# A KV-cache decode kernel: the last kept unit of a row's first pass moves behind all units scored ahead, ten of twelve V's instead of twelve run ahead of the kept K's, fewer V's are loaded in halves, and there are five sets of p

## The chip, the cores and the metric

The kernel runs on one core of a Trainium2 chip. The metric is device microseconds of one execution. A core has TensorE (PE; its weight loads are shown as PEld), VectorE (DVE), ScalarE (ACT), GpSimd (POOL) and SyncE (SP), and 16 DMA engines that move data between HBM and the on-chip SBUF. In this kernel SP issues almost all loads; it waits in order, so a load whose target is not yet free holds back all loads behind it.

## The reference

There are 8 batch rows, each with one token of 448 values. Two layers run one after the other with the same weights and the same K and V caches: attention, MLP block, attention, MLP block. In short:

```
def A(x):                                   # attention over the cache
    q = (x @ wq).reshape(8, 1, 16, 256)
    scores = einsum("bhqd,bhkd->bhqk", q, repeat(k_cache, 2)) * 256 ** -0.5
    o = einsum("bhqk,bhkd->bhqd", softmax(scores), repeat(v_cache, 2))
    return o.reshape(8, 1, 4096) @ wo
def B(x):                                   # one token: the shifted mixer adds nothing
    x1 = x + hs                             # hs comes from rows of zeros
    return x1 + gelu(layernorm(x1) @ w3) @ w4
x = x + A(layernorm(x)); x = x + B(layernorm(x))
x = x + A(layernorm(x)); x = x + B(layernorm(x))
```

Each cache is (8 rows, 8 KV heads, 4096 positions, 256 values) in bf16, 134 MB. K and V of every row are needed twice, once in each pass, and a row's second pass needs its query, which depends on everything in its first pass. Rows don't depend on one another.

## The kernel before

**Units and items.** A unit (called a task in the code) is a pass (0 or 1), a row and a pair `gp` (0 to 3) of two KV heads. It has four K pieces and four V pieces of 1 MB each. The kernel writes out by hand one list, `items`, of 512 such pieces in the order in which they are used. A K item is transposed in 32x32 blocks on VectorE (`transpose_k`, L777) and multiplied with the query on TensorE (`scores`, L792; two K pieces that lie side by side are scored with one set of 32 matmuls instead of two); ScalarE then takes exponentials (L801). A V item is multiplied with the probabilities on TensorE (`pv`, L845, 16 matmuls). Before its first V, a unit's probabilities are transposed by four matmuls and a copy (`turn_p`, L828 and L835) into one of `NP` sets (`psv`, L114), and ScalarE copies the part for each V into `ptw` (L955).

**Places.** SBUF has 15 places of 1 MB. Pairs 2 and 3 are "kept": for the row in progress all eight K pieces and four V pieces of these two units stay in their places from the first pass to the second, and one V plus a quarter of another is set aside in PSUM (L812, L1086). At the moment when the first pass ends, 12 of 15 places are held and only three are left to stream through. `emit_loads` walks the load list in the order of `items` after each item and issues whatever has a place; `place_for` and `both_for` choose the place and hold two neighbours for the two halves of a K pair, in which case the second waits for its own place even if others are free. A V in the set `halved` is loaded as two DMAs of half a MB (L767), every other as one (L764); a pair of K's whose two places are both to be had goes as one DMA of 2 MB (L739).

**The chain of a row.** Between a row's first and second pass stand: denominators of the softmax, scaling of the output (L476), the product with wo (L365), a norm (L235, L254), the MLP (L383, L365), another norm, the product with wq (L316) and the spreading of the query (L335). It is a generator, advanced a step at a time by `step`. So that loads go on meanwhile, units of other rows, whose queries are there already, are scored ahead, and their V's are left over (`due`). The first `AFTER` = 12 of these go into `items` right behind the first pass; they are called `narrow`. While a narrow V is used, one step of the chain is taken in the middle of its 16 matmuls and one after them. A step that yields 2 makes the chain skip one turn, if the item is in `loose`. Here the three free places are a ring: a place is loaded, used and loaded again.

**The order.** `block(k, v)` puts the four K's of unit k and among them what is due. `first_kept` (L581 on) writes the first pass of a row's two kept units k2 and k3 together with the units scored ahead (four of them, so 16 V's, in rows 0 to 3; three, so 12 V's, in rows 4 to 7). In it, the last unit scored ahead comes after k3. The second pass then begins with the kept K's, which need no load; scoring two of them frees two places. V's that are due beyond the twelve stand among these.

Of the kernel before, what the change touches and what calls it, by code (L numbers as in the profile page):

```python
# [8 lines left out]
FP32 = mybir.dt.float32  # L9
BF16 = mybir.dt.bfloat16  # L10
U32 = mybir.dt.uint32
ACT = mybir.ActivationFunctionType
ALU = mybir.AluOpType
# [4 lines left out]
def kernel(  # L18
# [27 lines left out]
    nc = tc.nc  # L46
# [5 lines left out]
    Hq = HD // Dh  # L52
# [5 lines left out]
    HC = F // 128  # L58
    scale_exp = float(Dh) ** -0.5

    NC = 15
    NP = 4

    kept = [(gp, 0, n) for gp in (GP - 1, GP - 2) for n in range(4)]
    kept += [(GP - 1, 1, n) for n in range(1, 4)] + [(GP - 2, 1, 2)]
# [6 lines left out]
    chn = ctx.enter_context(tc.tile_pool(name="chn", bufs=1))  # L72
# [10 lines left out]
    MID = Bn // 2  # L83
# [126 lines left out]
    def norm(x, nb, twice):  # L210
# [19 lines left out]
        nc.vector.tensor_reduce(  # L230
            xs, xx.rearrange("p s f b -> p s b f"), mybir.AxisListType.X, ALU.add
        )
        yield 2
        st = room_ps("st", nb).rearrange("p (s b) -> p s b", b=nb)
        nc.tensor.matmul(st, ones, xs, start=True, stop=True)  # L235
        yield 0
# [71 lines left out]
    def project_q(b0, nb, qT):  # L308

        yield from norm(xT[:, :, b0 : b0 + nb], nb, False)  # L310
        q_ps = room_ps("q", nb).rearrange("p (c b) -> p c b", b=nb)
        for j in range(2):
            for h in range(Hq):
                for fc in range(4):
                    w, xi = wblk(wq_sb, HD, 2 * h + j, fc)
                    nc.tensor.matmul(  # L316
                        q_ps[:, j * Hq + h, :],
                        w,
                        xbs(nb)[:, xi, :],
                        start=(fc == 0),  # L320
                        stop=(fc == 3),
                    )
                if h % 8 == 7:
                    yield (2, 0)[j] if h == Hq - 1 else None
        nc.vector.tensor_copy(qT, q_ps)  # L325
        yield

# [48 lines left out]
    def mlp_hidden(b0, nb):  # L376

        yield from norm(xT[:, :, b0 : b0 + nb], nb, True)
        h_ps = room_ps("h", nb)
        for c in range(HC):  # L380
            for fc in range(4):
                w, xi = wblk(w3_sb, F, c, fc)
                nc.tensor.matmul(  # L383
                    h_ps[:, c * nb : c * nb + nb],
                    w,
                    xbs(nb)[:, xi, :],
                    start=(fc == 0),
                    stop=(fc == 3),
                )
            if c % 7 == 6:  # L390
                yield 0 if c == HC - 1 else None
        g_t = chn.tile([128, 2, HC * MID], FP32, tag="g")
        hh, g0 = g_t[:, 0, 0 : HC * nb], g_t[:, 1, 0 : HC * nb]
        if nb == 1:
            HT_t = chn.tile([128, HC, 1], BF16, tag="HT")
            HT = HT_t[:]
        else:
            HT = HTw[:, :, b0 : b0 + nb]

        nc.vector.tensor_scalar_mul(hh, h_ps, 0.5)  # L400
        nc.vector.scalar_tensor_tensor(g0, hh, 2 * 0.044715, h_ps, ALU.mult, ALU.mult)
        nc.vector.scalar_tensor_tensor(g0, g0, 1.0, h_ps, ALU.add, ALU.mult)
        nc.scalar.activation(g0, g0, ACT.Tanh, scale=0.7978845608028654)
        yield 0
        nc.vector.scalar_tensor_tensor(
            HT,
            g0.rearrange("p (c b) -> p c b", b=nb),
            1.0,
            hh.rearrange("p (c b) -> p c b", b=nb),
            ALU.add,  # L410
            ALU.mult,
        )
        yield 2
        return HT
# [150 lines left out]
    AFTER = 12  # L565
# [21 lines left out]
    def first_kept(b, units, before):  # L587

        k2, k3 = ((0, b, gp) for gp in keep)
        todo = list(units)  # L590
        block(todo.pop(0), before)
        if len(todo) > 2:
            block(todo.pop(0))
        block(k2)
        block(todo.pop(0), k2) if todo else block(None, k2)
        block(k3)
        block(todo.pop(0), k3) if todo else block(None, k3)
        assert not todo
        items.extend(due)
        due.clear()  # L600
        for u in units:
            due.extend((number[u], 1, c) for c in range(4))
        narrow.update(due)
        if len(due) >= AFTER:
            loose.update(due)
        halved.update(due[: AFTER + 2])
        items.extend(due[:AFTER])
        del due[:AFTER]

    block((0, 0, free[0]))  # L610
    block((0, 0, free[1]), (0, 0, free[0]))
# [284 lines left out]

    def add_gen(kind, g, at=0, until=0, total=0, main=False):
        gens.append(
            {"kind": kind, "g": g, "at": at, "until": until, "n": 0, "of": total, "skip": 0, "main": main}
        )  # L900

    alone = []
# [1 line left out]
    def step(idx, calm=False, kinds=("chain", "last", "rest")):  # L904

        for kind in kinds:
# [3 lines left out]
            if alone and idx < len(items) and kind != "rest" and not e.get("locks"):  # L910
                if kind == "last" or not any(m["main"] for m in gens):
                    continue
            if calm and e["skip"] and items[now[0]] in loose:
                e["skip"] -= 1
                continue
            if not e["of"] or e["n"] < e["of"] * (idx - e["at"] + 1) / max(e["until"] - e["at"], 1):
                e["n"] += 1
                had = len(locked)
                got = next(e["g"], gens)
                while calm and got == 0:  # L920
                    got = next(e["g"], gens)
                if len(locked) != had:
                    e["locks"] = len(locked) > had
                e["skip"] = 1 if got == 2 else 0
                if got is gens:
                    gens.remove(e)

# [242 lines left out]
```

## Time and profile before

| | |
|---|---|
| Time, median of 3 runs | 1092.21 us (1091.31 to 1095.92) |
| The profiled execution: its own time | 1093.14 us |
| The profiled execution: span | 1091.3 us |
| Mean granted TensorE clock | 0.586 |
| Moved by DMA | 438.29 MB, 402 GB/s on average |
| Busy: PE, PEld, DVE, ACT, POOL | 673.7, 421.5, 605.6, 160.5, 16.3 us |

No engine is busy for more than 62% of the span, while the load queue of SP is busy for 98.3% of it, as the mean of 16 DMA engines. The row of GB/s in 40 slices of the span is the one to read: it moves between 374 and 427 in the body of the kernel, and where it dips there are chains. A window of a few microseconds gives the same number for any stretch.

### The profile page before, as it was taken

Reading aid. Unit: us, or ns where it says so; the run is one execution under the profiler, and the core shown is the slowest. Engines: PE = TensorE matmul, PEld = TensorE weight load, DVE = VectorE, ACT = ScalarE, POOL = GpSimd, SP = SyncE. Lnnn points to the kernel's source line nnn. Section 1 sums busy time; section 2 is a strip of 40 time slices with the busy share of each in tenths; the row PEclk is TensorE's granted clock in tenths of the full one; section 3 lists DMA queues with packets and bytes.
Section 4 is the critical chain, followed back from the end, with each engine's and each line's share of the span. In section 5 each row is a group of like instructions: output and inputs, shape, how many; then the busy total and the mean of one; then the engine's idle time right before and its main releaser. Section 6 shows DMA issues by size and latency. Waiting matters only on the chain.

```text
span 1091.3 us, 30928 instructions
## 1 busy us (share of the span) xinstructions
PE 673.7 (62%) x13836; PEld 421.5 (39%) x13836; DVE 605.6 (55%) x1266; ACT 160.5 (15%) x612; POOL 16.3 (1%) x27
## 2 busy tenths in 40 slices
PE   3244457943777348764587537764776467756785
PEld 2122234522445124432254324542454244533555
DVE  4357841597318872288623873289327941795181
ACT  0011111211112111111101211111111111111120
POOL 0000000000000000000000000000000000000000
PEclk9995555565556555565555655556556555655565
DMA  9999999999999999999999999999999999999994
GB/s 357 394 427 426 420 393 398 419 425 426 374 411 424 425 408 393 402 425 420 398 393 420 421 423 385 395 418 426 392 382 422 423 380 377 426 416 394 400 420 186
DMA packets 71509, 438.29 MB, mean 402 GB/s; under 512 B 7624, under 2 KB 11600, under 8 KB 40016
## 3 DMA queue, kind: packets, MB, share of 16 engines
q1 hardware_dynamic: 71184, 435.94, 98.3%
q8 instruction: 108, 1.77, 0.6%
q10 hardware_dynamic: 192, 0.38, 0.1%
q14 instruction: 25, 0.20, 0.0%
HBM read 436.28 MB, written 0.01 MB: 400 GB/s over the span
## 4 chain that ended last, share of the span: by engine, by line
DMA 61%; PE 19%; DVE 13%; SPq 3%; issue 2%; ACT 2%; POOL 0%; DVEq 0%; ACTq 0%
DMA places<-in_A_v_cache_dram 40%; DMA places<-in_A_k_cache_dram 19%; DVE places L777 10%; PE sc L792 8%; PE o L845 6%; SPq L174 2%; PE misc L365 2%; DVE store L812 1%; PE misc L476 1%; SPq L764 1%; ACT p_n L801 1%; DVE places L819 1%; DMA wq_sb<-in_A_wq_dram 1%; PE misc L383 1%; PE misc L316 1%
## 5 line engine op out<-in xcount | busy, mean ns | idle before, releaser
L777 DVE STREAM_TRANSPOSE places<-places 128x512 uint32<-128x512 uint32 (+1 forms) x576 | 456.5, 854 | 87.2 <-DMA places<-in_A_k_cache_dram 79.0
L792 PE MATMUL sc<-places,qbd 128*8 128x128 bf16 (+1 forms) x5440 | 257.8, 342 | 228.4 <-DVE places L777 215.9
L845 PE MATMUL o<-places,ptw 128*8 128x256 bf16 x3968 | 253.7, 385 | 145.6 <-DMA places<-in_A_v_cache_dram 113.7
L792 PEld LDWEIGHTS <-qbd 128*8 128x8 bf16 x5440 | 139.7, 106 | 304.6 <-DVE places L777 137.8
L845 PEld LDWEIGHTS <-ptw 128*8 128x8 bf16 x3968 | 99.7, 99 | 226.4 <-issue 135.3
L801 ACT ACTIVATE p_n<-sc 128x256 bf16<-128x256 f32 x128 | 95.1, 743 | 390.6 <-PE sc L792 390.6
L955 ACT COPY ptw<-psv 128x32 bf16<-128x32 bf16 x248 | 50.1, 225 | 187.9 <-PE o L845 163.3
L440 DVE RECIPROCAL rz<-misc 128x8 f32<-128x8 f32 (+1 forms) x35 | 6.4, 184 | 101.7 <-PE misc L437 44.3
L835 ACT CAST psv<-misc 128x128 bf16<-128x128 f32 x64 | 17.0, 265 | 267.9 <-PE misc L828 267.9
L365 PEld LDWEIGHTS <-wo_sb 128*128 128x128 bf16 x1280 | 38.8, 105 | 17.7 <-issue 17.5
L316 PEld LDWEIGHTS <-wq_sb 128*128 128x128 bf16 x1152 | 33.6, 104 | 24.0 <-issue 13.9
L476 PE MATMUL misc<-R_t,o_sb 128*128 128x8 f32 (+1 forms) x132 | 30.7, 342 | 11.4 <-ACT o_sb L470 5.9
L472 DVE MEMSET o<- 128x256 f32 x33 | 9.0, 272 | 49.8 <-PE o L845 39.2
L476 PEld LDWEIGHTS misc<-R_t,o_sb 128*128 128x128 f32 x132 | 27.9, 293 | 21.5 <-ACT o_sb L470 12.3
L339 DVE CAST qbd<-misc 32x64 bf16<-32x64 f32 x104 | 22.4, 215 | 22.0 <-PE misc L335 20.9
L801 ACT ACTIVATION_READ_ACCUMULATOR p_n<-sc 128x1 f32 x128 | 33.7, 264 | 0.0
L365 PE MATMUL misc<-OT,wo_sb 128*128 128x1 bf16 x1024 | 31.9, 166 | 2.5 <-DVE zs_t L426 2.5
L316 PE MATMUL misc<-xb,wq_sb 128*128 128x1 bf16 x1024 | 32.6, 166 | 0.3 <-issue 0.3
L325 DVE CAST qT<-misc 128x32 bf16<-128x32 f32 x8 | 1.5, 192 | 55.0 <-PE misc L316 55.0
L254 POOL TENSOR_TENSOR t<-t,nhalf 128x2 f32<-128x2 f32 (+2 forms) x20 | 14.0, 703 | 1062.4 <-DVE t L275 1062.4
L437 PEld LDWEIGHTS misc<-zm,one 128*128 128x128 f32 x70 | 16.0, 285 | 12.1 <-issue 7.5
L383 PEld LDWEIGHTS <-w_sb 128*128 128x128 bf16 x560 | 16.8, 105 | 10.0 <-issue 9.5
(104 smaller groups left out, 313.5 us busy)
## 6 DMA issues: line engine op xcount, KB each, us to landing
places<-in_A_k_cache_dram SPq DMA_DIRECT2D x53, 2048.0 KB, 21.1
places<-in_A_v_cache_dram SPq DMA_DIRECT2D x210, 512.0 KB, 7.4
places<-in_A_v_cache_dram SPq DMA_DIRECT2D x103, 1024.0 KB, 17.2
places<-in_A_k_cache_dram SPq DMA_DIRECT2D x86, 1024.0 KB, 13.9
places<-in_A_v_cache_dram SPq DMA_DIRECT2D x8, 768.0 KB, 7.5
wo_sb<-in_A_wo_dram SPq DMA_DIRECT2D x1, 3584.0 KB, 27.0
wq_sb<-in_A_wq_dram SPq DMA_DIRECT2D x3, 1024.0 KB, 9.6
w_sb<-in_B_w_dram SPq DMA_DIRECT2D x1, 1568.0 KB
```

What stands on the lines that cost most here:

```text
L174: nc.sync.dma_start(t[:, fc * cols : (fc + 1) * cols], src[fc * 128 : fc * 128 + 128, :])
L316: nc.tensor.matmul(q_ps[:, j * Hq + h, :], w, xbs(nb)[:, xi, :], start=(fc == 0), stop=(fc == 3),)
L339: nc.vector.tensor_copy(qbd[32 * a : 32 * a + 32, :, :, a, :], qs.rearrange("p e (f g u h) -> p (e f) u g h", f=2, u=2, h=2)[:, :, u],)
L365: nc.tensor.matmul(y_ps[:, fc, :], w[:, i, at : at + 128], rhs(i), start=start, stop=stop, skip_group_check=open is not None,)
L383: nc.tensor.matmul(h_ps[:, c * nb : c * nb + nb], w, xbs(nb)[:, xi, :], start=(fc == 0), stop=(fc == 3),)
L476: nc.tensor.matmul(ot_ps[:, j], o_sb[:].rearrange("p (i j) -> p j i", j=2)[:, j], R, start=True, stop=True)
L777: nc.vector.transpose(w, w)
L792: nc.tensor.matmul(sc[32 * k : 32 * k + 8, 128 * x : 128 * (x + nx)], qbd[:, ep, gp].rearrange("p a h -> p (a h)"), v, start=(n == 0), sto ...
L801: nc.scalar.activation(p_sb[:, :, :, 2 * u : 2 * u + 2].rearrange("p t i x -> p x t i"), sc[:, 256 * u : 256 * u + 256].rearrange("p (x t ...
L835: nc.scalar.copy(p_to, pt_ps.rearrange("p t k (a h) -> p a (t k) h", a=4))
L845: nc.tensor.matmul(o_ps[32 * q : 32 * q + 8, :], ptz[:, at : at + 8], v[:, y * Dh : (y + 1) * Dh], start=False, stop=(y >= 12), skip_group ...
L955: nc.scalar.copy(ptw[:, ring_of[it], :, 6:8], psv[slot_of[it[0]]][:, it[2]])
```

## The change

The order in `first_kept` changes: all units scored ahead now stand before k3, the last kept unit, whose four K's and four V's are the last loads before the ring. The number n of V's put right behind the first pass is the smaller of 12 and two less than are due: 12 of 16 in rows 0 to 3 as before, and 10 of 12 in rows 4 to 7, where the other two now stand behind the first two kept K's of the second pass. Only the first n - 2 of the V's ahead are loaded in halves: 10 instead of 14 in a row of 16, 8 instead of 12 in a row of 12. More units hold probabilities at once, so there are five sets of p; the room comes from the MLP's scratch tile `g`, whose second part moves, for four rows at once, into PSUM. The MLP's two products now read the halved value from SBUF twice instead of the original from PSUM, with the constants changed accordingly. Skipped turns are renumbered: a step that yields 2 always skips the next, one that yields 3 only in `loose`, which now holds only where n is 12. The steps that yield 3 are the norm before its matmul and the second of four parts of the product with wq.

```
-    NP = 4
+    NP = 5
...
         block(k2)
-        block(todo.pop(0), k2) if todo else block(None, k2)
+        block(todo.pop(0), k2)
+        if todo:
+            block(todo.pop(0))
+        assert not todo
         block(k3)
-        block(todo.pop(0), k3) if todo else block(None, k3)
-        assert not todo
-        items.extend(due)
-        due.clear()
+        block(None, k3)
         for u in units:
             due.extend((number[u], 1, c) for c in range(4))
+        n = min(AFTER, len(due) - 2)
         narrow.update(due)
-        if len(due) >= AFTER:
+        if n == AFTER:
             loose.update(due)
-        halved.update(due[: AFTER + 2])
-        items.extend(due[:AFTER])
-        del due[:AFTER]
+        halved.update(due[: n - 2])
+        items.extend(due[:n])
+        del due[:n]
...
-        yield 2
+        yield 3
...
-                    yield (2, 0)[j] if h == Hq - 1 else None
+                    yield (3, 0)[j] if h == Hq - 1 else None
...
-            if calm and e["skip"] and items[now[0]] in loose:
-                e["skip"] -= 1
+            if calm and e["skip"]:
+                e["skip"] = False
                 continue
...
-                e["skip"] = 1 if got == 2 else 0
+                e["skip"] = got == 2 or (got == 3 and items[now[0]] in loose)
...
-        g_t = chn.tile([128, 2, HC * MID], FP32, tag="g")
-        hh, g0 = g_t[:, 0, 0 : HC * nb], g_t[:, 1, 0 : HC * nb]
+        g_t = chn.tile([128, HC * MID], FP32, tag="g")
+        hh = g_t[:, 0 : HC * nb]
+        g0 = g_t[:, HC : 2 * HC] if nb == 1 else misc[:, 448 : 448 + HC * nb]
...
-        nc.vector.scalar_tensor_tensor(g0, hh, 2 * 0.044715, h_ps, ALU.mult, ALU.mult)
-        nc.vector.scalar_tensor_tensor(g0, g0, 1.0, h_ps, ALU.add, ALU.mult)
-        nc.scalar.activation(g0, g0, ACT.Tanh, scale=0.7978845608028654)
+        nc.vector.scalar_tensor_tensor(g0, hh, 4 * 0.044715, hh, ALU.mult, ALU.mult)
+        nc.vector.scalar_tensor_tensor(g0, g0, 1.0, hh, ALU.add, ALU.mult)
+        nc.scalar.activation(g0, g0, ACT.Tanh, scale=2 * 0.7978845608028654)
```

More of the change, by code (lines that the diff above doesn't have):

```diff
@@ L898, in add_gen @@
         gens.append(
-            {"kind": kind, "g": g, "at": at, "until": until, "n": 0, "of": total, "skip": 0, "main": main}
+            {"kind": kind, "g": g, "at": at, "until": until, "n": 0, "of": total, "skip": False, "main": main}
         )
```

## The prediction

> **What bounds the kernel now.** First the page: queue, chain and issues.
>
> ```profile
> DMA  9999999999999999999999999999999999999994
> GB/s 357 394 427 426 420 393 398 419 425 426 374 411 424 425 408 393 402 425 420 398 393 420 421 423 385 395 418 426 392 382 422 423 380 377 426 416 394 400 420 186
> q1 hardware_dynamic: 71184, 435.94, 98.3%
> ...
> DMA 61%; PE 19%; DVE 13%; SPq 3%; issue 2%; ACT 2%; POOL 0%; DVEq 0%; ACTq 0%
> ...
> places<-in_A_v_cache_dram SPq DMA_DIRECT2D x210, 512.0 KB, 7.4
> places<-in_A_v_cache_dram SPq DMA_DIRECT2D x103, 1024.0 KB, 17.2
> ```
>
> The queue is full throughout, yet its rate dips to 374 to 400 at regular distances. The question is what one MB costs in the dips. So next the table of stretches, around the chains of row 1 (first three), row 4 (next four) and row 6 (columns: stretch, length, busy time of PE, PEld, DVE, ACT, POOL, granted clock, DMA share, GB/s):
>
> ```profile
> 195.00:265.00 70.00, 43.29 (x864) 26.15 (x864) 56.79 (x93) 11.90 (x43) 0.00 (x0) 0.57 1.01 424
> 265.00:295.00 30.00, 16.02 (x296) 9.42 (x296) 12.98 (x30) 4.05 (x17) 0.70 (x1) 0.56 0.97 381
> 295.00:320.00 25.00, 19.58 (x413) 11.56 (x407) 3.75 (x21) 2.76 (x13) 0.55 (x1) 0.50 1.03 412
> 580.00:650.00 70.00, 40.49 (x841) 25.45 (x830) 49.13 (x84) 11.77 (x44) 0.00 (x0) 0.60 1.01 422
> 650.00:670.00 20.00, 12.50 (x234) 7.41 (x235) 10.04 (x20) 3.18 (x15) 0.00 (x0) 0.59 0.96 377
> 670.00:690.00 20.00, 15.66 (x340) 9.63 (x335) 4.04 (x24) 2.02 (x10) 1.25 (x2) 0.50 1.03 409
> 690.00:725.00 35.00, 26.23 (x594) 19.34 (x586) 16.90 (x43) 6.36 (x22) 0.00 (x0) 0.51 1.01 402
> 910.00:925.00 15.00, 11.36 (x232) 7.06 (x233) 1.38 (x7) 2.52 (x9) 0.00 (x0) 0.50 0.96 349
> ```
>
> Away from chains the queue moves 423 GB/s. Each chain has three parts: the end of the first pass (381, 377), the ring of halved V's (412, 409: slower, though the share is above 1), and, in rows 4 to 7, the end of the ring (349). Time lost against 423 is length x (1 - rate/423). The ends of pass: 3.0 us in row 1, 2.2 in row 4; the same view over all eight (150:165 at 377, 400:420 at 371, 530:550 at 376, 765:780 at 379, 872:892 at 368, 988:1005 at 383) sums to **17.2 us**. The stretches behind them sum to **16.2**: 5.7 in rows 0 to 3, 10.4 in rows 4 to 7, of which the ring's ends (690:725, 800:812 at 339, 910:925, 1025:1037 at 387) make 1.7 + 2.4 + 2.6 + 1.0 = 7.7. Nothing else is to be had but the start and the 15 us behind the last load, which the change leaves alone.
>
> Why the end of a pass is slow, the timeline of row 1 shows:
>
> ```profile
> 257.90 17.08 SPq L764 DMA_DIRECT2D places<-in_A_v_cache_dram  x3
> ...
> 268.32 4.74 DVE L777 STREAM_TRANSPOSE places<-places 128x1024 uint32<-128x1024 uint32 x6 [3.99 <-DMA places<-in_A_k_cache_dram]
> ...
> 271.93 1.02 PE L792 MATMUL sc<-places,qbd 128*8 128x256 bf16 x16 [7.16 <-DVE places L777]
> ...
> 273.11 1.02 PE L792 MATMUL sc<-places,qbd 128*8 128x256 bf16 x16
> ...
> 275.70 38.19 SPq L767 DMA_DIRECT2D places<-in_A_v_cache_dram  x28
> ```
>
> SP issues one V at 257.9 and the next two at 274.2: they need a place of the K pair scored last, which lands at 268.2, is transposed for 4.7 us and scored until 274.1. By then the queue has run out.
>
> **The change, part by part.** *Order.* Counting MB issued and not yet used, item by item over the last twelve items of row 1's first pass, the program before has 8 8 7 6 4 6 6 4 3 5 4 3, the changed one 4 10 9 10 8 8 6 6 6 5 4 3. The dip to 4 moves to where the unit ahead is scored, so I follow that one. SP's queue before: kept K's, K pair ahead, kept V0, K pair ahead, kept V1 to V3, ring. After: K's ahead, two pairs of kept K's, kept V0 to V3, ring. The second kept pair waits for a place of the first K pair ahead. That pair lands about 254.3, where the kept pair landed that it replaces (its transposes start at 254.34), and is scored at 260.1; behind it stand one V, two K's and a pair: 3 x 2.48 + 4.9 = 12.3 us of transfer, so the order comes 6.5 us before the queue is empty. The next three V's and two ring V's go out by 265, with some 18 us queued. Kept K's land by 273.1, are transposed by 278, scored by 279; exponentials, `turn_p` (0.3 + 0.3 + 0.25 us, now here) and four V's at 1.1 us let the chain start at 285.5, where it started at 284.1. So PE enters the ring late by 1.2 us, and its first V's, whose transfers are then ordered 5.2 to 5.8 us ahead of landing, lose some 0.5 us. Of the mean 17.2/8 = 2.15 us lost per row, I leave 0.3 for halves (ten of each stretch's microseconds at 409 instead of 423), 0.5 for this and 0.35 for DMA engines out of step, and take 1.0. Bounds: 0, since landings and not engine averages count, and 1.85. **-8 us** for eight rows (0 to -14.8).
>
> *Ten of twelve.* In rows 4 to 7 the chain goes through nine V's instead of ten. PE there:
>
> ```profile
> 684.59 1.01 PE L316 MATMUL misc<-xb,wq_sb 128*128 128x1 bf16 x32
> ...
> 686.93 0.27 PE L828 MATMUL misc<-identb,p_n 128*128 128x32 bf16 x4
> 687.81 1.03 PE L845 MATMUL o<-places,ptw 128*8 128x256 bf16 x16 [0.60 <-ACT ptw L955]
> 688.77 1.01 PE L316 MATMUL misc<-xb,wq_sb 128*128 128x1 bf16 x32
> ```
>
> A V with two parts of wq is 1.2 + 2.0 = 3.2 us of PE against 2.55 of transfer, and `turn_p` with its wait (0.27 + 0.60) comes on top just here; the fifth set of p lets that be done earlier, among kept K's. My sum of PE over nine V's: 9 x 1.2, two parts of wo and four of wq at 1.0, four of the MLP at 0.9, two norms and L476 at 0.6, query 0.4: 23 us, against 9 x 2.55 = 23. PE is level with the queue: the dropped skips cost two waits of 0.3 us for VectorE, and PE is about 1.5 us late at the end; I charge 0.5 us a row (0 to 2). For it, the first kept K's are scored (1.9 us, no load) two V's sooner, and their places take two loads before, not behind, the last V's. Before, three loads at the ring's end were each ordered some 3.8 us before the queue ran out (behind them a V of 2.55 and 768 KB of 1.87, less 0.65 for using the second half); now one is. Of 7.7 us I take 3.5 back (0 to 6), net **-1.5 us** (+8 to -6).
>
> *Halves.* 104 halved V's become 72 in these stages, so 32 fewer issues. At 412 a MB takes 2.545 us, at 423 2.479: 32 x 0.066 = 2.1 us. But a whole V is ordered only when both halves of its place are used, and cannot be used from its middle. Whole V's that followed the last step of a chain kept up (one ordered at 316.1 landed 6.9 us later, with no gap). About three in each row now stand behind parts of wq. The one such case in the trace, the 768 KB load ordered at 691.88, landed 0.7 us later than its size asks. I take 0.05 us each, 1.1 us; **-1 us** (-2.1 to 24 x 0.7 - 2.1 = +14.7).
>
> The Trainium skill's "DMA: Bandwidth & Descriptors", section "Anatomy of one DMA", puts a transfer at 2.0 us + bytes/436e3 (fitted on GpSimd's path, not SP's). By it 32 V's joined would save 32 x 2.0 = 64 us; but it also says that the semaphore waits for the last byte, and by the same formula a whole V is first usable 1.2 us later than its half, 38 us against the change. The row at 412 GB/s, with 28 halves queued one behind another, shows neither in full: the fixed part is hidden as long as orders come early.
>
> *At nothing.* Five score pairs more lie side by side: 64 matmuls take 1.93 us, 32 wide ones 1.88. The MLP edits keep their 0.17 us operations on VectorE, which is idle in the ring; in the tail, four of them read or write PSUM instead: +-0.3 us. 34 issues fewer on SP at 0.33 to 0.43 us: SP waits anyway.
>
> Sum: -8 - 1.5 - 1 = -10.5 us on the execution of 1093.14, 1082.6; it stood 0.9 over the median, so **1081.7 us**.
>
> **Rivals.** *No change (1087 to 1093):* the starved time is shared out anew. For it: between 270 and 290 the DMA share is 0.90 to 0.98 even while starved, so engines out of step may set the landings, and order gives little; row 1's ring V's land only some 1.4 us later than back-to-back transfers would. Price: 0.3 us a row from order, and 1 from halves: 1092.2 - 3.4 = 1089. Against it: the 16.3 us without an issue.
>
> *Slower:* whole V's in a three-place ring. One mechanism: with the chain's step between its two halves, a whole V keeps its place 0.6 + 1.0 + 0.6 us after landing instead of 0.6, so its successor is ordered too late. At 0.7 us for each of 24 it costs 16.8, against gains of 8 + 1.5 + 2.1: 1092.2 + 5.2 = 1097. It decides above 0.5 us a V. For it: that 768 KB load. Against: most whole V's come behind the chain's last step.
>
> *The chain in nine V's overruns the ten:* PE does not finish the query before the kept K's; each of four rows then waits with three places full for two parts of wq, 2 us a row: 1081.7 + 8 = 1090.
>
> **How the numbers follow.** A measurement tells 0.5%, 5.5 us, from no change. Forecast 0.63 (1075 to 1086), no change 0.12, overrun 0.09, slower 0.16 (1092 to 1099). Faster is the forecast plus a little of the two middle cases, 0.66; same 0.19; slower 0.15. The range goes from 1075 (order at 1.85 us a row) to 1096, just short of the slower rival's value.
>
> **What would show it.** Right: in the stretches that correspond to 265:295 and 650:670 the rate rises from 380 to 400 or more; SP has no gap of 16 us before the last kept V's; halves 146, whole V's 135, pairs 55; the ends of rows 4 to 7 above 385. Wrong: whole V's at the ring's end landing 3 us or more apart; PE waiting for VectorE or the query when the kept K's begin; a new gap of SP where the unit ahead is scored.

## The result, and the profile after

The changed kernel takes 1085.77 us (median; 1083.99 to 1086.46), against 1092.21 us (1090.28 to 1096.31) of the kernel before: a ratio of 0.993, with a 95% interval of 0.9902 to 0.9957. It is faster by 6.4 us; 10.5 us were forecast. The profiled execution of it took 1086.46 us with a span of 1084.6 us, 6.7 us less than the one before; its mean granted clock was 0.598 (0.586). The clock does not explain the difference: over the 76 executions of the kernel before that stand beside the experiments it lies between 0.567 and 0.657, and the time does not follow it (correlation -0.09).

The page of the changed kernel, queue, chain and issues:

```profile
GB/s 355 393 427 425 425 409 387 417 424 425 408 385 425 426 421 408 386 425 422 421 398 407 423 424 406 376 423 424 409 385 426 423 409 384 422 424 404 377 421 186
q1 hardware_dynamic: 66288, 435.94, 98.4%
...
DMA 51%; PE 23%; DVE 18%; SPq 3%; issue 2%; ACT 2%; POOL 0%; DVEq 0%; ACTq 0%
...
places<-in_A_v_cache_dram SPq DMA_DIRECT2D x135, 1024.0 KB, 16.1
...
places<-in_A_v_cache_dram SPq DMA_DIRECT2D x146, 512.0 KB, 7.4
```

The same 435.94 MB in fewer packets, with the queue as busy as before. The dips in the rate have moved: two neighbouring slices at 374 and 411 have become 408 and 385. The table of stretches of the changed kernel (columns as in the prediction; the last two are DMA share and GB/s) says where:

```profile
265.00:295.00 30.00, 17.75 (x344) 10.60 (x337) 13.44 (x32) 4.90 (x18) 0.70 (x1) 0.56 1.01 411
295.00:320.00 25.00, 17.54 (x382) 10.90 (x381) 3.49 (x20) 2.86 (x13) 0.55 (x1) 0.54 0.99 378
...
650.00:670.00 20.00, 14.18 (x268) 8.45 (x261) 8.89 (x25) 4.16 (x16) 0.70 (x1) 0.59 1.02 412
670.00:690.00 20.00, 15.72 (x364) 10.30 (x365) 3.77 (x21) 1.42 (x7) 0.55 (x1) 0.50 0.98 371
690.00:725.00 35.00, 24.45 (x518) 16.48 (x511) 19.89 (x45) 6.88 (x26) 0.00 (x0) 0.60 1.00 410
910.00:925.00 15.00, 11.52 (x193) 8.14 (x195) 5.27 (x16) 3.82 (x14) 0.00 (x0) 0.50 1.01 416
```

The ends of pass rose from 381 and 377 to 411 and 412, the ends of the ring from 402 and 349 to 410 and 416. But the rings themselves (295:320, 670:690) fell from 412 and 409 to 378 and 371.

**Where the time went.** With the prediction's measure, length x (1 - rate/423), summed over the eight ends of pass, the eight rings (165:195, 295:320, 420:460, 550:580, 670:690, 780:800, 892:910, 1005:1025), the four ring's ends, and two stretches of the next pass (725:765, 925:988), in us; the windows stand still while the stages shift by some microseconds, and each row is one execution. Experiments 1 and 2 differ only in rows 4 to 7, and yet the stretches of rows 0 to 3 lose 10.4 us in one and 13.8 in the other, so a sum is good to 2 or 3 us:

| | ends of pass | rings | ring's ends | next pass | sum | span |
|---|---|---|---|---|---|---|
| before | 17.2 | 8.4 | 7.8 | 0.3 | 33.7 | 1091.3 |
| after | 5.4 | 19.7 | 2.3 | 0.4 | 27.8 | 1084.6 |
| order alone (second experiment) | 12.4 | 11.6 | 3.5 | 4.0 | 31.5 | 1088.6 |
| after, halves back (first) | 10.1 | 13.1 | 0.7 | 0.6 | 24.5 | 1081.4 |
| no halves (fifth) | 3.8 | 29.4 | 7.7 | 1.7 | 42.6 | 1108.2 |
| no halves, steps behind (ninth) | 6.0 | 24.2 | 6.9 | 0.2 | 37.3 | 1095.1 |
| no halves, four places (tenth) | 3.5 | 6.9 | 1.5 | 0.0 | 11.9 | 1088.4 |
| ten everywhere (eleventh) | 7.0 | 13.2 | 0.6 | 0.6 | 21.4 | 1077.9 |

The sum fell by 5.9 us and the span by 6.7. So the change won 17.3 us at the ends (11.8 and 5.5) and gave 11.3 back in the rings.

What it won is the end of SP's wait. In the view of SP's waits between 250 and 300 us, the kernel before has

```profile
SPq L764 <- DVE places L777: 12.5, 1, 12.5
```

one wait of 12.5 us, behind which the last kept V's stood (columns: us in total, times, longest). In the changed kernel SP waits for the transposes there as well, but before a K pair and at most 5.5 us:

```profile
SPq L741 <- DVE places L779: 8.8, 2, 5.5
```

What it lost is seen in the timeline of TensorE in row 1 of the changed kernel, at the end of the ring (start, length, instruction, idle time before it):

```profile
311.56 1.02 PE L847 MATMUL o<-places,ptw 128*8 128x256 bf16 x16 [2.23 <-DMA places<-in_A_v_cache_dram]
314.05 1.02 PE L847 MATMUL o<-places,ptw 128*8 128x256 bf16 x16 [1.47 <-DMA places<-in_A_v_cache_dram]
...
316.64 1.02 PE L847 MATMUL o<-places,ptw 128*8 128x256 bf16 x16
319.52 0.61 PE L847 MATMUL o<-places,ptw 128*8 128x256 bf16 x16 [1.85 <-DMA places<-in_A_v_cache_dram]
```

These are whole V's; they land at 311.52, 314.01, 316.60 and 319.48, that is 2.49, 2.59 and 2.88 us apart where a full queue needs 2.48. They were ordered 5.2, 4.7 and 4.0 us ahead of the landing before theirs. The later the order, the larger the gap.

### The profile page after: what moved, and what is told of

The parts are those of the page before. It is cut to its first block, busy times and chain, and to the rows that moved or that the text cites. A ratio compares the mean times of both kernels' runs of the same rounds, so it can differ in the third digit from the quotient of the medians.

```text
span 1084.6 us, 30554 instructions
## 1 busy us (share of the span) xinstructions
PE 659.6 (61%) x13676; PEld 418.6 (39%) x13676; DVE 606.5 (56%) x1266; ACT 163.8 (15%) x612; POOL 16.4 (2%) x27
## 3 DMA queue, kind: packets, MB, share of 16 engines
q1 hardware_dynamic: 66288, 435.94, 98.4%
## 4 chain that ended last, share of the span: by engine, by line
DMA 51%; PE 23%; DVE 18%; SPq 3%; issue 2%; ACT 2%; POOL 0%; DVEq 0%; ACTq 0%
DMA places<-in_A_k_cache_dram 26%; DMA places<-in_A_v_cache_dram 23%; DVE places L779 14%; PE o L847 8%; PE sc L794 7%; PE misc L365 3%; PE misc L477 2%; SPq L174 2%; SPq L766 1%; DVE places L821 1%; ACT p_n L803 1%; DVE store L814 1%; DMA wq_sb<-in_A_wq_dram 1%; PE misc L316 1%; DVE qbd L339 1%
## 5 line engine op out<-in xcount | busy, mean ns | idle before, releaser
L794 PE MATMUL sc<-places,qbd 128*8 128x128 bf16 (+1 forms) x5280 | 254.3, 342 | 244.5 <-DVE places L779 235.8
L847 PE MATMUL o<-places,ptw 128*8 128x256 bf16 x3968 | 243.4, 381 | 122.9 <-DMA places<-in_A_v_cache_dram 96.9
L794 PEld LDWEIGHTS <-qbd 128*8 128x8 bf16 x5280 | 135.9, 104 | 324.2 <-DVE places L779 157.9
L847 PEld LDWEIGHTS <-ptw 128*8 128x8 bf16 x3968 | 101.2, 101 | 193.1 <-issue 117.5
L477 PE MATMUL misc<-R_t,o_sb 128*128 128x8 f32 (+1 forms) x132 | 29.6, 334 | 11.6 <-ACT o_sb L471 6.6
L339 DVE CAST qbd<-misc 32x64 bf16<-32x64 f32 x104 | 22.4, 216 | 25.3 <-PE misc L335 24.2
L803 ACT ACTIVATION_READ_ACCUMULATOR p_n<-sc 128x1 f32 x128 | 33.7, 263 | 0.0
L830 PEld LDWEIGHTS <-p_n 128*128 128x128 bf16 x256 | 11.6, 105 | 29.1 <-issue 17.5
L830 PE MATMUL misc<-identb,p_n 128*128 128x32 bf16 x256 | 18.2, 191 | 6.8 <-ACT p_n L803 6.8
```

What stands on the lines that cost most here:

```text
L339: nc.vector.tensor_copy(qbd[32 * a : 32 * a + 32, :, :, a, :], qs.rearrange("p e (f g u h) -> p (e f) u g h", f=2, u=2, h=2)[:, :, u],)
L477: nc.tensor.matmul(ot_ps[:, j], o_sb[:].rearrange("p (i j) -> p j i", j=2)[:, j], R, start=True, stop=True)
L794: nc.tensor.matmul(sc[32 * k : 32 * k + 8, 128 * x : 128 * (x + nx)], qbd[:, ep, gp].rearrange("p a h -> p (a h)"), v, start=(n == 0), sto ...
L803: nc.scalar.activation(p_sb[:, :, :, 2 * u : 2 * u + 2].rearrange("p t i x -> p x t i"), sc[:, 256 * u : 256 * u + 256].rearrange("p (x t ...
L830: nc.tensor.matmul(pt_ps[:, t], p_sb[:, t].rearrange("p i x -> p (i x)"), cols, start=True, stop=True,)
L847: nc.tensor.matmul(o_ps[32 * q : 32 * q + 8, :], ptz[:, at : at + 8], v[:, y * Dh : (y + 1) * Dh], start=False, stop=(y >= 12), skip_group ...
```

## The experiments

Three questions: what is each part worth, why do whole V's cost, and is there a better mixture? The experiments ran in four groups, each beside the kernel before, whose median was 1091.8 to 1093.5 us; the ratios to it are what can be compared across groups. In the code cuts, ... stands for lines left out. Line numbers in the profiles are those of the kernel at hand: the matmuls of a V are L845 before, L847 in the changed kernel and L846 in some experiments.

**1. Halves put back.**

```
-        halved.update(due[: n - 2])
+        halved.update(due[: n + 2])
```

> The changed kernel with one part undone: again two more V's than are put ahead are loaded in halves (14 in a row of 16, 12 in a row of 12, where the changed one has 10 and 8). Theory W (whole V's in the three-place ring are ordered too late while steps of the chain stand between their halves, and that is why the rings of the changed kernel run at 364 to 389 GB/s): the rings come back to 400 or more and the time falls by 3 to 5 us under the changed kernel, to about 1081 to 1083 us. Theory P (PE enters the ring late and is level with the queue; halves or not is the same): rings stay below 390 and the small packets cost their 2 us: 1087 to 1088 us. Forecast's own term (halves -1 us): 1086 to 1087 us.

1082.21 us, 0.9906 (0.9887 to 0.9924): 3.6 us better than the changed kernel by the medians, 2.6 by the ratios, whose intervals overlap. The time is the one that theory W gave, but only part of the rings came back to about 400: in rows 0 to 4 they run at 397 to 407 GB/s, in rows 5 to 7 at 369, 374 and 390 (407 to 411 in the kernel before). So in those rows something else seems to cost as well; it comes up again in experiment 2. By the table the fewer halves lose 8.2 us in the rings and at their ends, and gain 4.7 at the ends of pass, which this edit does not touch; stages that moved across the fixed windows may be part of that. The sum of the three is 3.5 us.

**2. The order alone:** the changed kernel with the halves of before and twelve of twelve.

```
-        n = min(AFTER, len(due) - 2)
+        n = min(AFTER, len(due))
...
-        halved.update(due[: n - 2])
+        halved.update(due[: n + 2])
```

> The new order of units alone (with the fifth set of p and the scratch that it needs): twelve of twelve V's ahead and halves as in the kernel before. The forecast's term for the order was -8 us, so 1084 us against 1092.2. By the table of stretches the ends of pass gave back 11.8 us, so 1080 to 1082 us if the order causes nothing else. Theory P, with a late start of the ring as a consequence of the order, gives some of it back in the ring: 1085 us.

1087.17 us, 0.9953 (0.9935 to 0.9972): the order is worth 5 us, less than any of the three expectations (1080 to 1085 us) had. Against experiment 1, which differs in the ten of twelve, that part is worth another 5 (0.9906 against 0.9953). Where part of that lies was a surprise. Of this kernel, stretches, then SP, then VectorE, in the pass behind the chain of row 4:

```profile
745.00:750.00 5.00, 3.66 (x70) 2.20 (x73) 5.00 (x8) 0.77 (x3) 0.00 (x0) 0.50 0.85 313
```

```profile
724.07 14.89 SPq L766 DMA_DIRECT2D places<-in_A_k_cache_dram  x3
748.25 2.23 SPq L741 DMA_DIRECT2D places<-in_A_k_cache_dram  x2
```

```profile
745.07 10.45 DVE L779 STREAM_TRANSPOSE places<-places 128x1024 uint32<-128x1024 uint32 x13
```

and the same two views, stretches and SP, of experiment 1 (ten of twelve):

```profile
745.00:750.00 5.00, 0.32 (x12) 0.10 (x7) 2.44 (x4) 0.74 (x2) 0.00 (x0) 0.55 1.03 436
```

```profile
734.21 11.78 SPq L741 DMA_DIRECT2D places<-in_A_k_cache_dram  x3
```

With twelve of twelve, SP orders nothing for 9.3 us (738.96 to 748.25) while VectorE, busy for 5.00 of 5 us, is behind with its transposes, and the queue falls to 313 GB/s; with ten, the next pair is ordered before. In the table this is 4.0 against 0.6 us, and the ring's ends are 3.5 against 0.7. The loss does not stand in the kernel before (0.3): the order makes it, the ten of twelve take it away. Experiment 3, also with twelve of twelve, has it again: 4.4 us there against 0.4 in the changed kernel. But what the ring's ends gain is lost in the rings of rows 4 to 7: 7.3 us in experiment 1 against 3.8 here (9.5 in the changed kernel against 7.2 in experiment 3).

**3. The changed kernel with twelve of twelve,** and its 10 and 8 halved V's.

```
-        n = min(AFTER, len(due) - 2)
+        n = min(AFTER, len(due))
...
-        halved.update(due[: n - 2])
+        halved.update(due[: 10 if len(due) > AFTER else 8])
```

> The changed kernel with twelve of twelve V's ahead again in rows 4 to 7 (the first eight still in halves), and with it the skipped turns as before. If ten of twelve is worth what the ends of rings show (5.5 us back in rows 4 to 7) and its price is paid elsewhere, the time is 1089 to 1091 us. If the squeeze of the chain into nine V's costs as much in the rings of rows 4 to 7 as it gives back at their ends (6.8 against 5.5 us in the stretches), the time is the same as the changed kernel's, 1085 to 1086 us.

1090.0 us, 0.9968 (0.9949 to 0.9988), as expected if the ten of twelve are worth what they show. Against the changed kernel: ten of twelve is worth 4 us here too. Against experiment 2: fewer halves cost 1.6 us by the ratios, 2.8 by the medians.

**4. The kernel before with fewer halves.**

```
-        halved.update(due[: AFTER + 2])
+        halved.update(due[: 10 if len(due) > AFTER else 8])
```

> The kernel before with one part alone: 10 V's of 16, and 8 of 12, in halves. Forecast's term: -1 us, 1091 us (from -2.1, small packets saved and nothing else, to +14.7). Theory W: slower by 3 us or more, 1095 us or more, with more where steps of wq stand between the halves of rows 4 to 7, whose chains take ten V's here. Theory P: 1090 to 1091 us.

1096.78 us, 1.0041 (1.0024 to 1.0057): fewer halves cost 4.5 us (2.6 to 6.2) by themselves, as theory W had it. So the sign of this term was wrong. With the new order the two comparisons (experiments 1 and 3) point the same way, but each difference is too small for its intervals.

**5. No halves at all,** which makes the disputed cost large.

```
-        halved.update(due[: n - 2])
```

> The changed kernel, with none of the V's of these rings in halves: the 72 that it still loads as two halves come as one DMA of 1 MB. Theory P (big packets pay, as the forecast had it: 0.066 us a V saved, little lost): 72 x 0.066 = 4.8 us faster than the changed kernel, about 0.988 to 0.990 of the kernel before. Theory W (a whole V in the three-place ring is first usable late and gives its place up late; undoing 32 whole V's was worth 3.5 us, 0.11 us each): 72 x 0.11 = 8 us slower than the changed kernel, about 1.000 of the kernel before, and more if the cost rises with each V that stands behind another late one. Under W the gigabytes per second of the rings, 364 to 398 in the changed kernel, fall below 370 in most rows.

1106.78 us, 1.0139 (1.0109 to 1.0169), 21 us over the changed kernel and so 0.29 us for each of 72 further whole V's; more than the 0.11 us that theory W took (it allowed for more where late V's follow one another). The rings of three rows in this kernel:

```profile
165.00:195.00 30.00, 19.96 (x450) 13.01 (x443) 3.77 (x21) 2.88 (x13) 0.56 (x1) 0.55 0.96 351
295.00:320.00 25.00, 16.40 (x372) 10.87 (x376) 5.04 (x28) 1.86 (x9) 1.25 (x2) 0.50 0.94 342
420.00:445.00 25.00, 18.95 (x388) 11.98 (x384) 5.10 (x29) 2.57 (x12) 1.25 (x2) 0.50 0.93 351
```

**6 and 7. A shorter step in the middle of a V,** with the changed kernel's halves and with the halves put back:

```
-                for fc in range(4):
+                for fc in range(4) if nb > 1 else (0,):
...
-                        stop=(fc == 3),
+                        stop=(fc == 3 or nb == 1),
```

> The changed kernel, but the product with wq of a single row uses only the first of four blocks of the inner dimension, 8 matmuls a part instead of 32; three quarters of that product are left out. Each of the four parts on TensorE should shrink from 1.0 to about 0.25 us, 3 us a row less between the V's of a ring. Theory S (whole V's cost because the chain's step stands between their two halves, so that the place is given up late and the next order comes late): the cost of the whole V's shrinks with the step, so this is faster than the changed kernel by 3 us or more, about 0.989, and only up to 1 us slower than the same with the halves put back. Theory L (the whole V itself is the cost: its first half can't be used until the second has landed, whatever stands between): it is as far behind the one with halves put back as before, 3 to 4 us. Where PE itself was level with the queue, both gain alike and the gap decides.

> The changed kernel with the short product with wq (8 matmuls a part instead of 32, three quarters of that product left out) and with as many V's in halves as in the kernel before. Theory S: within 1 us of the short product with fewer halves, since there is little left between the halves. Theory L: 3 to 4 us faster than that one. If PE in the ring bounds nothing, it equals the changed kernel with the halves put back, about 0.9906 of the kernel before; if PE was level with the queue in rows 4 to 7, it is faster than that by 2 us or more.

1082.66 us, 0.9911 (0.988 to 0.9941), and 1079.3 us, 0.9884 (0.9857 to 0.9911). Both gain 2 to 3 us from the shorter product, and the gap stays at 3.4 us (2.9 by the ratios), as theory L has it. But the gap has an interval of some 4 us to each side, and of the four V's of a row that are whole in the one and halved in the other, only two stand in the ring beside the chain. So this does not refute theory S.

**8. The skipped turns in all rows,** on top of experiment 1.

```
-        if n == AFTER:
-            loose.update(due)
-        halved.update(due[: n - 2])
+        loose.update(due)
+        halved.update(due[: n + 2])
```

> The changed kernel with the halves put back and with the skipped turns of the chain in all rows, also where ten of twelve V's run ahead (the changed kernel drops two of them in rows 4 to 7). Theory D (dropping the skips makes PE wait for VectorE in the middle of the ring, 0.2 to 0.5 us at four places in row 4): these waits are gone, and four rows gain up to 1 us each, 0.988 to 0.990 of the kernel before against 0.9906 with the halves put back alone. Theory O (two skips more make the chain overrun the ten V's, so that the kept K's wait for the query): 1 to 2 us a row slower, 0.994 to 0.998.

1080.1 us, 0.9892 (0.9868 to 0.9917). Theory O (1 to 2 us a row slower) falls: the chain fits into nine V's with the skips as well. The ratio lies where theory D put it, but that the dropped skips cost something is not shown, since the interval overlaps that of experiment 1. In the table of stretches the rings of rows 4 to 7 lose 4.1 us here against 7.3 in experiment 1, which points to the dropped skips; experiment 11, which skips too, loses 6.4. The waits themselves are small. In row 4 of the changed kernel TensorE waits for VectorE at four places (0.53, 0.59, 0.32 and 0.23 us), of which one of 0.30 us is left in experiment 8. The two longest:

```profile
666.92 0.59 PE L235 MATMUL misc<-t,one 128*128 128x2 f32 x2 [0.53 <-DVE t L230]
...
669.31 1.05 PE L383 MATMUL misc<-xb,w_sb 128*128 128x1 bf16 x28 [0.59 <-DVE xb L283]
```

**9. No halves, and both steps of the chain behind a V** instead of one in its middle.

```
                     ring_of[it],
-                    (lambda: step(idx, True)) if it in narrow else None,
+                    None,
...
         step(idx, it in narrow)
+        if it in narrow:
+            step(idx, True)
```

> No V of the rings in halves, and both steps of the chain taken behind the 16 matmuls of a V instead of one in their middle, so that nothing stands between the two halves of a whole V and its place is given up about 1.0 us sooner. The same kernel with a step in the middle took 1106.8 us, 21 to 24 us more than those with halves. Theory S (the step between the halves is the cost): most of that goes, 1085 to 1092 us. Theory L (the whole V itself: three places of 1 MB leave an order only 2 x 2.48 us less the time the V is held, under the 4 us that landings in these traces need): at most a third goes, 1099 to 1106 us.

1096.69 us, 1.0039 (1.0017 to 1.006). Ten of the 21 to 25 us go: more than a third, less than most. Both theories miss, and the timelines of TensorE in row 1 show what they have in common. With a step in the middle (experiment 5):

```profile
306.65 0.60 PE L846 MATMUL o<-places,ptw 128*8 128x256 bf16 x8 [2.16 <-DMA places<-in_A_v_cache_dram]
307.18 0.59 PE L235 MATMUL misc<-t,one 128*128 128x2 f32 x2
307.69 0.60 PE L846 MATMUL o<-places,ptw 128*8 128x256 bf16 x8
...
316.11 0.60 PE L846 MATMUL o<-places,ptw 128*8 128x256 bf16 x8 [2.07 <-DMA places<-in_A_v_cache_dram]
```

and with both behind (experiment 9):

```profile
303.56 1.02 PE L846 MATMUL o<-places,ptw 128*8 128x256 bf16 x16 [1.15 <-DMA places<-in_A_v_cache_dram]
304.51 1.86 PE L316 MATMUL misc<-xb,wq_sb 128*128 128x1 bf16 x64
...
308.87 1.03 PE L846 MATMUL o<-places,ptw 128*8 128x256 bf16 x16 [0.47 <-DMA places<-in_A_v_cache_dram]
```

In the first, the V begun at 306.65 holds its place for 1.6 us (2.1 us where the step is a part of wq). The V that takes its place was ordered at 308.34, 3.4 us before the landing ahead of it (311.77), and came 1.8 us late: it is the one that PE begins at 316.11. In the second a V holds its place for 1.0 us, the V's of this stretch are ordered 4.1 to 4.5 us ahead, and they come up to 0.4 us late.

So it is the lead of an order that counts, from the order to the landing ahead of it. The table is worked out from the issue and landing times of all loads of 0.5 and 1 MB in the fourteen traces, issued between 60 and 1060 us, where the landing ahead is recorded too (lateness is the time between the two landings, less 1.27 or 2.48 us for 0.5 or 1 MB):

| lead, us | 1 MB: loads | median late, us | mean | over 0.25 us late | 0.5 MB: loads | median | over 0.25 us late |
|---|---|---|---|---|---|---|---|
| under 3 | 15 | 0.54 | 0.67 | 60% | 0 | | |
| 3 to 4 | 45 | 0.40 | 0.58 | 60% | 1 | 1.02 | |
| 4 to 5 | 83 | 0.01 | 0.21 | 22% | 39 | -0.01 | 25% |
| 5 to 8 | 106 | 0.00 | 0.16 | 20% | 574 | 0.00 | 8% |
| over 8 | 747 | 0.00 | 0.04 | 5% | 170 | 0.01 | 3% |

An order that comes less than 4 us ahead is late in six cases of ten, by a median of 0.4 to 0.5 us. A ring of three places with whole V's gives it 2 x 2.48 us less the time that a V is held, 1.2 us or, with a step of 1 us in the middle, 2.2: a lead of 3.8 or 2.8 us, as long as nothing lands late; where landings are 2.70 and 2.88 us apart, as in experiment 9 above, the lead behind them is longer, 4.5 us. The same ring with halves gives 5 x 1.27 us less 0.6 to 1.6: 4.7 to 5.7.

The Trainium skill's "DMA: Bandwidth & Descriptors", in its section "Anatomy of one DMA", gives a fixed part of about 2.0 us, most of it the receipt of the last byte, for GpSimd's path. No run here shows that part alone; by it the estimate would be that a lead of 2 us is enough, and the table above asks for about twice as much on SP's queue.

**10. No halves, and a fourth place for the ring,** by keeping one V piece of a row fewer.

```
-    kept += [(GP - 1, 1, n) for n in range(1, 4)] + [(GP - 2, 1, 2)]
+    kept += [(GP - 1, 1, n) for n in range(1, 4)]
...
-        halved.update(due[: n - 2])
```

> No V of the rings in halves, and one V piece of a row fewer kept, so that four places instead of three stream through the ring; that piece is loaded again in the second pass, 8 MB more in all, 8 x 2.48 = 20 us more transfer. Theory L (an order must come about 4 us before the landing ahead of it, and three whole places can't give that, four can): the rings, at 342 to 375 GB/s with three places, come to 410 or more; about 20 us of starving go and 20 us of transfer come, 1100 to 1110 us with a mean rate above 404 GB/s. Theory R (whole V's are slow for another reason, such as PE's work between them): the rings stay below 385 GB/s and the time is 1120 us or more.

1093.2 us, 1.0008 (0.9993 to 1.0023): 13.6 us faster than with three places (14 by the ratios), and faster than theory L had put it, though it moves 446.58 MB, 8.3 MB more, which take 19.7 us at 423 GB/s. So 33 us of starving went (31 in the table). The same three rings:

```profile
165.00:195.00 30.00, 21.98 (x488) 14.72 (x484) 4.59 (x25) 4.00 (x17) 0.56 (x1) 0.61 1.01 419
295.00:320.00 25.00, 20.11 (x441) 13.07 (x441) 3.77 (x21) 2.85 (x13) 0.55 (x1) 0.50 1.01 416
420.00:445.00 25.00, 20.14 (x432) 12.94 (x428) 5.63 (x32) 2.30 (x11) 1.25 (x2) 0.50 1.01 405
```

From 342 to 351 they rise to 405 to 419 (over all eight rows 394 to 419, so not everywhere the 410 of theory L), with whole V's and with the chain's step in their middle. Theory R falls. The loads of 1 MB in the two traces, as far as the landings are recorded (about half), say the same: in experiment 5, 21 of them were ordered less than 4 us ahead, and these make 15.3 of 22.3 us of lateness; in experiment 10 none was, and the lateness is 4.0 us. So whole V's cost not by their size, nor by the step alone, but by too little lead in three places.

**11. Ten V's ahead in every row,** on top of experiment 8.

```
-    AFTER = 12
+    AFTER = 10
```

> The changed kernel with the halves put back, the skipped turns in all rows, and ten V's ahead of the kept K's also in the four rows that have 16 due (they had twelve). Theory K (kept K's sooner refill the ring: ten of twelve was worth 4 to 5 us in four rows): the other four rows gain 0.5 to 1 us each, 1076 to 1078 us, 0.985 to 0.988 of the kernel before. Theory N (in those rows 16 V's are due and the chain's steps no longer fit into the ring; the kept K's wait for the query): 1082 us or more.

1079.57 us (1076.95 to 1080.62), 0.9874 (0.9849 to 0.99). By its ratio this is the best version: the new order, ten V's ahead in all rows, all of these and two more in halves, the skips everywhere. It beats the kernel before by 1.3% and the changed kernel by some 6 us. Theory N falls. The step from experiment 8 (0.9892) by itself lies within the intervals.

**12. The same with both steps behind a V,** as in experiment 9.

> Ten V's ahead in every row, halves put back, skipped turns in all rows (1079.6 us, 0.9874 of the kernel before), and now both steps of the chain taken behind a V's matmuls, none in their middle. With no halves, the same move gained 10 us, since whole V's were ordered 2.8 to 3.8 us ahead of the landing before theirs, under the 4 us that an order needs. Theory L: a half is ordered 4.7 to 5.7 us ahead, above 4 us with the step in the middle too, so the move gains nothing: within 2 us, 0.986 to 0.989. Theory S (a step between two uses of a place always delays the ring): 3 us or more are gained, 0.9845 or less.

1088.01 us, 0.9966 (0.995 to 0.9982): 8.4 us slower than experiment 11 by the medians, 10 by the ratios, where one theory had no change and the other a gain. The move has a price of its own that neither had. The product with wq in the timeline of TensorE, with a step in the middle (experiment 11):

```profile
301.68 1.01 PE L316 MATMUL misc<-xb,wq_sb 128*128 128x1 bf16 x32
302.62 0.60 PE L846 MATMUL o<-places,ptw 128*8 128x256 bf16 x8
303.16 1.01 PE L316 MATMUL misc<-xb,wq_sb 128*128 128x1 bf16 x32
```

and with both behind (experiment 12):

```profile
303.06 0.60 PE L846 MATMUL o<-places,ptw 128*8 128x256 bf16 x8 [0.99 <-DMA places<-in_A_v_cache_dram]
303.59 1.86 PE L316 MATMUL misc<-xb,wq_sb 128*128 128x1 bf16 x64
305.39 1.03 PE L846 MATMUL o<-places,ptw 128*8 128x256 bf16 x16
```

Two steps in a row keep PE for 1.86 us, longer than the 1.27 us in which a half lands, and the kept K's begin 1.9 us later in row 1 (311.47 against 309.58), of which 1.0 us was there when the chain began. By the measure of the table the ring's ends lose 5.6 us here against 0.6, and the rings 16.8 against 13.2. That the later kept K's are the cause fits, but was not tested alone. If the move has such a price with whole V's too, the step in the middle is worth more of the 21 to 25 us of experiment 5 than the 10 that experiment 9 shows; that stays open.

## Why the prediction was right, and where not

The sign and the range were right: 1085.77 us lies in 1075 to 1096. The size was not: of 10.5 us, 6.4 came. The three terms, by the ratios (each to some 2 to 4 us):

| term | forecast | measured | from |
|---|---|---|---|
| order | -8 | -5 (-3 to -7) | experiment 2 |
| ten of twelve | -1.5 | -4 to -5 | experiments 1 against 2, changed kernel against 3 |
| fewer halves | -1 | +1.6 to +4.5 | experiments 1, 3, 4 |
| sum | -10.5 | -7.6 by the ratio, -6.4 by the medians | the changed kernel |

The last row is no test of the other three: the experiments go from the kernel before to the changed one in steps, so the differences along one path add up to it by themselves. That the time fell into the range is in part luck. The order brought some 3 us less than forecast and the halves some 3 to 5 us less, and the ten of twelve, some 3 us better than forecast, made up for part of it.

**The order: right in mechanism, mis-sized.** The wait of SP went, as foreseen, and the ends of pass rose above 400 GB/s in seven of eight rows (383 became 396 in the last). The step that failed is "take 1.0" of 2.15 us a row for what the order recovers: it looked only at the ends of pass. There the changed kernel gained 11.8 us, more than the 8 (7.1 with the halves back). But alone (in an execution 3 us over its median) the order gained 4.8 us at the ends of pass and 4.3 at the ring's ends, lost 3.2 in the rings, and the next pass lost 3.7 us, in a place that the working had not looked at: SP waiting behind transposes with VectorE full. Some 1.9 us of what lacks at the ends of pass are of that one execution: in row 0 it ran at 341 GB/s where experiment 1, alike up to there, ran at 394. The 1.2 us by which PE was to enter the ring late did not come: the scaling of the output began at 284.28, 0.5 us sooner than before.

**Ten of twelve: right in sign, too small by a factor of three.** The 3.5 us at the ring's ends came as 2.8 (experiment 1 against 2) to 5.5 (changed kernel against experiment 3), as argued from the kept K's that give places back sooner. But in the same traces the rings of rows 4 to 7 lost 3.5 and 2.3 us more, about as much as the 2 us charged for a chain squeezed into nine V's, so rings and their ends together came out 0.7 us worse in the first pair of runs and 3.2 better in the second. Whether the squeeze or the dropped skips make that loss stays open; the chain does fit, since experiment 8 puts still more turns into the same V's. What the forecast did not have at all is the next pass, which gained 3.4 to 4.0 us: there the ten of twelve repair what the order breaks. The forecast had left this at nothing without a reason, and it is the gain that both pairs of runs show.

**Halves: wrong in sign.** The step that failed reads "Whole V's that followed the last step of a chain kept up", and from it that only some three V's in a row would come late, at 0.05 us each over 24 (which is 1.2 us, not 1.1). The V taken for it, ordered at 316.1, had a lead of 4.4 us (the landing ahead was at 320.5): a single whole V in a ring of halves, whose place came free from a halved V with no step in the middle. In the ring the lead of whole V's shrinks from one to the next (5.2, 4.7, 4.0 us in row 1); the one with 4.0 us took the place of a whole V that had been used in one piece, with no step in its middle, and still came 0.40 us late. Counting the 2.1 us that bigger packets save by the forecast, the 32 V's lost 3.7 to 6.6 us, 0.12 to 0.21 us each; with no halves at all it is more.

**The rivals.** The slower rival named the right kind of place: a whole V in a three-place ring is ordered too late. It put its price at 0.7 us a V and the point from which it decides at 0.5; over 32 V's it was 0.12 to 0.21 (0.15 to 0.28 over its 24), so the halves took a sixth to a half of the gain of the other two parts and not the sign. Its mechanism was one half: the chain's step between the halves makes it worse (experiment 9), but three places of 1 MB are short of lead without it. "No change" falls with the changed kernel's ratio, 0.9957 at most (1087.5 us). The chain did not overrun: in row 4 the query was spread by 686.5 us, and PE waited 1.33 us for a V before it began the kept K's at 689.06; in rows 5 to 7 the spreading ended 2 to 3 us before the kept K's began.

**What was to show it.** As said for right: 146 halves, 135 whole V's and 55 pairs; the ring's ends in rows 4 to 7 at 410, 391, 416 and 422; no gap of 16 us. As said for wrong: whole V's nearly 3 us apart in row 1 (2.88). PE did not wait for VectorE or the query when the kept K's began, as seen. SP had a new gap of 6.7 us where the unit ahead is scored (from 253.9 to 260.6 us in row 1), but the pair that ended it came some 6.5 us ahead, as the forecast had it (worked back from the landing of the V behind it at 274.51), and the queue ran at 425 GB/s from 255 to 270 us.

## What to carry to other kernels

In a ring of few buffers count the lead: the time from an order to the landing of the load ahead of it, which is what the other buffers still have to receive less the time that a buffer is held. If that is near the time below which landings in the trace come late (4 us here), smaller pieces win, though each byte costs more in them; more buffers win too, and make the large pieces cheap. When a wait is taken away at one place, run the same table of stretches over the rest of the pass before summing, since the place where the work now piles up may be a whole stage further on.

## What the runs showed that was not expected

- A starved queue looks busy. In the rings of the changed kernel the DMA share stays at 0.98 and 0.99 while the rate falls to 371 and 378 GB/s. The trace's packets show why: between 300 and 320 us the median packet of 8192 bytes took 309 ns, as away from the chains (311), but the mean was 346 (313 away from the chains), and the longest 2.15 us. So part of the lost time stands in the trace as the time of a few long packets and counts as busy; the rate is to be read and not the share.
- Where a load in halves costs 159 ns for 4096 bytes against 309 for 8192 (3% more per byte), the halves still won in a ring of three places: the kernel with none was slower by 21 to 25 us.
- Some 5% of the loads of 1 MB ordered more than 8 us ahead were over 0.25 us late as well, by up to 1.5 us. No run here tells why.
